# Another order of issue for one recurrent-attention and mixer kernel

## The chip, the core and the metric

The kernel runs on one core of one Trainium2 chip. The metric is the device time of one execution in microseconds (us). Five engines work side by side, each on its own queue and in the order of that queue: TensorE (PE, matmuls), VectorE (DVE), ScalarE (ACT), GpSimd (POOL) and SyncE (SP, which here issues nearly all transfers). They wait for one another by semaphores.

## The reference

Two blocks follow each other: a recurrent attention with a decaying state, and an MLP-mixer block whose input is the attention's output.

```python
def _attn_ref(r, k, v, w, u):          # (4, 8, 768, 48) each, u (8, 48)
    for t in range(S):
        cur = einsum('bhd,bhe->bhde', u[None] * kt, vt)
        y[:, :, t] = einsum('bhd,bhde->bhe', rt, state + cur)
        state = wt[:, :, :, None] * state + einsum('bhd,bhe->bhde', kt, vt)

def _moe_ref(x, w_tok1, w_tok2, w_ch1, w_ch2):     # x (4, 768, 384)
    h = np.maximum(x.transpose(0, 2, 1) @ w_tok1, 0.0) @ w_tok2
    u = x + h.transpose(0, 2, 1)
    return u + np.maximum(u @ w_ch1, 0.0) @ w_ch2
```

## The kernel before

The sequence of 768 steps of each of the 4 batches is cut into three **units** (`UB`) of two chunks of 128 steps, 12 units (`NU`) in all. Unit `i` is a set of **steps** with names, and the texts below write them as `i.name`:

- `ends` and `begins` (DVE): scans over the decay `w`, lines L435 and L443; `keys` and `queries` (DVE, L440 and L446): the keys and queries times these.
- `own0` to `own3` (ACT, L331): the keys times `u`; `own` (PE, L315): their products with the queries; `put` (DVE, L458): the diagonal of these into the tile `at`.
- `tokens` (PE, L345): the keys turned; `copied0`, `copied1` (ACT, L350): the copies of that out of PSUM; `carry` (PE, L365): keys times values into `kv_ps`.
- `by0` to `by3` (ACT, L501) and `up0` to `up3` (in the first three units PE, L508; later DVE): the state carried on over four blocks of 64 steps, each from the one before.
- `gram` (PE, L315) and `mask` (DVE, L327): keys times queries, the part below the diagonal into `at`.
- `before` (PE, L380), `seen` (ACT, L389), `after` (PE, L401): the output from the state and from `at`; `taken0` to `taken2` (ACT, L407): its copy into `x`.
- `small` and `large` (ACT, L427): whether the scan left a range of numbers that is safe.

Beside the units stand the steps of the mixer. Its weights come as words that are taken apart on the chip: `t0` to `t2` are pieces of the first two weights, `c0` to `c8` of the other two, each with `load` (SP, L261), `plus` and `minus` (ACT, L264 and L267), `lead`, `two`, `value`, `sum` (DVE, L270 to L281). The mixer of the first batch is plain: `h0` to `h11` (PE, L947), `relu0` and `relu1` (ACT, L950), `back0` to `back5` (PE, L958, and an addition on DVE, L960), `turn0` to `turn5` (PE, L969, and a copy on ACT, L971), `up` (PE, L993) and `down` (PE, L1004). The mixers of batches 1 to 3 work with split numbers (L667 to L820), take part of the weights from DRAM through a ring of ten slots, and have POOL add one of three forms.

What sets the order is written into the program. The first stage, up to the first three units and `h11`, is one list of steps in a call of `strict`; the rest is merged from ten streams by the digits of the string `ORDER`, a digit naming the stream whose next step comes. `strict` binds every instruction of a step behind the one before it on its engine, so that no scheduler moves it:

```python
for ins in block.instructions[done:]:
    if ins.engine in in_turn:
        if in_turn[ins.engine]:
            tc.add_manual_dep(ins, in_turn[ins.engine], no_sync, reason="order of issue")
        in_turn[ins.engine] = ins.name
```

`behind(gate, f)` makes a transfer wait until the step `gate` has ended. PSUM tiles are few: in the first stage the products `own`, `gram` and `before` share two places (`tag="gram"`), so the third waits until the first has been read, by `put`, `mask` or `taken`. Afterwards six banks go round.

Of the kernel before, what the change touches and what calls it, by code (L numbers as in the profile page):

```python
# [26 lines left out]
UB = C // UC  # L27
NU = B * UB
A = H // 2
# [18 lines left out]
SHRINK = (1.0 - 1.0 / BASE) ** 2  # L48
LEAST, MOST = 2.0 ** -40, 2.0 ** 40
MID = 3 * G // 4 * SEG1  # L50
ORDER = (
    "888008088078808800000888484440800840804080880808804844088488400448088408008888080080884808884040488844488888084840880880"
    "808840880808084448484008800080858808005000458500505588854545558485085848785005080558505855588400558085800005606068606846"
    "860600685786865658688606668086688566668868066800064869889466550048096660988848898089000484488044008000848080000018444141"
    "404040044004000000007000000404000440020000040550000050500000000000000005024200200045005020000555542000002004001224540105"
    "100550500055000750000000055050502000000500004500006624606000520000666506507606600506566660066600060066066606000000000000"
    "006405041104010500004006511611111661096012294296211041111044222990403443439223340234000004000010011000000400000007040000"
    "400040004004000400400000404000055000550000000000000000000005544000050000000000500014511000000000400000004555500545554000"
    "570550000450000000505550060000600066000506665000000665005600000000000066500001666656650661160651610000600006662106266212"
    "191166106100991111112002023393229933300002000001000110000000000000000000000000000000000000000000000000000000000000000000"  # L60
    "00000000000070001011000000000000000000000000000000000000000000000000000000000000000000000000000000000"
)


# [1 line left out]
def rwkv6_then_mixer(  # L66
# [25 lines left out]
    def behind(gate, f):  # L92

        def g():
            done = len(block.instructions)
            f()
            tc.add_manual_dep(block.instructions[done], ended[gate], wait, reason="time of issue")

        return g

    def strict(*fs):

        for f in fs:
            done = len(block.instructions)
            f()
            ended[f] = block.instructions[-1].name
# [5 lines that stand above are left out]
# [66 lines left out]
    def load_w(i):  # L178
        if i < NU:
            for cols in (slice(MID, WCOLS), slice(0, MID)) if i == 0 else (slice(0, WCOLS),):  # L180
                sp.dma_start(w_of(i)[:, cols], w[i][:, cols])
# [4 lines left out]
    def load_part(i, n):  # L186
        for rows in (slice(0, 128),) if i < UB else (slice(0, D), slice(P, P + D)):
            sp.dma_start(rk_of(i)[rows, ts(n, COLS)], rk[i, n, rows, :])

    def load_rk(i):  # L190
        if i < NU:
            for n in (1, 0):
                load_part(i, n)
# [3 lines left out]
    def load_v(i):  # L197
        if i < NU:
            vs[i] = vpool.tile([128, UC, DM], f32, name="vt", tag=f"vt{i % 2}")
            b, j = divmod(i, UB)  # L200
            sp.dma_start(vs[i], v[b, ts(j, UC * 128), :].rearrange("(c p) e -> p c e", p=128))
# [207 lines left out]
    def unit(i):  # L409
# [123 lines left out]
        def each(f, n):  # L533
            return [lambda m=m: f(m) for m in range(n)]

        return dict(ranges=each(ranges, 2), ends=ends, keys=keys, begins=begins, queries=queries, own_u=each(own_u, A),
                    own_gram=own_gram, copied=each(copied, UC), taken=each(taken, 3),
                    own_put=own_put, products=[lambda n=n: products(n) for n in range(3)], sums_put=sums_put,
                    tokens=tokens, gram=gram, mask=mask, carry=carry, before=before, seen=seen, after=after,
                    scaled=[lambda c=c, j=j: scaled(c, j) for c in range(UC) for j in range(2)],  # L540
                    updates=[lambda c=c, j=j: update(c, j) for c in range(UC) for j in range(2)])
# [476 lines left out]
    def attention_pieces(i):  # L1018

        e = units[i]  # L1020
        up, by, sums = e["updates"], e["scaled"], e["products"]
        k = lambda *names: tuple((i, n) for n in names)
        last = lambda *names: tuple((i - 1, n) for n in names) if i > UB else ()

        def piece(f, name, *ops):
            return (i, name), f, ops

        back = i // UB - 2
# [8 lines left out]
        loads = piece(lambda: load_rk(i + 1), "loads", ("Q", 8.0, last("before", "gram", "tokens")))  # L1037
        ends = piece(e["ends"], "ends", ("DVE", 2.6, last("small", "large", "by3", "w")))
        keys = piece(e["keys"], "keys", ("DVE", 1.25, k("ends") + last("loads")))
        small, large = (piece(e["ranges"][n], name, ("ACT", 1.4, k("ends"))) for n, name in enumerate(("small", "large")))  # L1040
        begins = piece(e["begins"], "begins", ("DVE", 2.35, k("ends")))
        tokens = piece(e["tokens"], "tokens", ("PE", 0.9, k("keys") + last("carry"), "k0", "k1"))
        copied = [piece(e["copied"][n], f"copied{n}", ("ACT", 0.6, k("tokens")), ("free", f"k{n}")) for n in range(2)]
# [31 lines left out]
    def interleaved(order, *streams):  # L1075
# [9 lines left out]
    raw_words.append(turned["xT"].rearrange("p m t -> p (m t)").bitcast(u32)[:, :4 * PIECE])  # L1085
    to_tok = conversion(("wtok1", "wtok2"), words_tok, rooms=lambda n: ((0, 1, 3)[n], n % 2))
    to_ch = conversion(("wch1", "wch2"), words_ch, rooms=lambda n: (n % 2, n % 2) if n else (2, 2))
    e0, e1, e2 = (unit(i) for i in range(UB))
    (_, p0, n0, lead0, two0, put0, add0), (_, p1, n1, lead1, two1, put1, add1), (_, p2, n2, lead2, two2, put2, add2) = to_tok
    _, p3, n3, lead3, two3, put3, _ = to_ch[0]  # L1090
    in_turn.update({pe.engine: None, dve.engine: None, act.engine: None, sp.engine: None})
    s0, s1, s2 = (e["updates"] for e in (e0, e1, e2))
    t0, t1, t2 = (e["scaled"] for e in (e0, e1, e2))
    strict(lambda: load_part(0, 1), masks, e0["ends"], e0["own_u"][0], e0["own_u"][1], e0["own_u"][2], e0["own_u"][3], e0["begins"],
           lambda: load_part(0, 0), e0["keys"], lambda: load_part(1, 1), e0["own_gram"], lambda: load_v(0), e0["ranges"][0], lambda: load_w(1),
           e0["tokens"], e0["queries"], e1["own_u"][0], e1["own_u"][1], e0["copied"][0], lambda: load_w(2), e0["gram"], e1["ends"], e0["copied"][1],
           lambda: load_part(1, 0), e0["carry"], e1["own_u"][2], s0[0], e0["own_put"], e1["own_u"][3], e0["ranges"][1], t0[1], s0[1],
           behind(e0["tokens"], to_tok[0][0]), e1["begins"], behind(e1["ends"], lambda: load_part(2, 1)), e1["own_gram"], t0[2], e1["keys"],
           e2["own_u"][0], s0[2], e2["own_u"][1], e1["own_put"], t0[3], e1["tokens"], behind(e0["tokens"], lambda: load_part(2, 0)),
           e0["before"], e2["own_u"][2], e0["mask"], e1["copied"][0], p0, e0["seen"], s0[3], e2["own_u"][3], behind(t0[2], lambda: load_v(1)),  # L1100
           e2["ends"], e1["copied"][1], t1[0], e0["after"], e0["taken"][0], e1["carry"], n0, to_tok[1][0], s1[0], e1["queries"], e0["taken"][1],
           e2["keys"], lead0, t1[1], e2["own_gram"], two0, s1[1], e0["taken"][2], e2["own_put"], e2["tokens"], t1[2], put0, e2["copied"][0],
           s1[2], t1[3], e2["copied"][1], e1["gram"], s1[3], e1["before"], t2[0], p1, add0, lambda: load_v(2), e1["mask"], e2["carry"], e1["seen"],
           h[1], s2[0], h[0], e2["ranges"][0], e2["begins"], behind(t1[1], to_tok[2][0]), t2[1], n1, h[3], e2["queries"], s2[1], lead1, two1,
           e1["after"], t2[2], s2[2], put1, e2["gram"], behind(e1["gram"], to_ch[0][0]), h[2], e1["taken"][0], e1["taken"][1], t2[3], e1["taken"][2],
           behind(t2[3], lambda: load_w(3)), p2, add1, e2["mask"], lambda: load_v(UB), behind(e2["own_gram"], to_ch[1][0]), e2["before"], h[4],
           e2["seen"], n2, e2["after"], lead2, two2, h[5], e2["taken"][0], h[6], e2["taken"][1], put2, e2["taken"][2], h[7], h[8], p3,
           h[10], add2, n3, behind(e1["tokens"], to_ch[2][0]), lead3, two3, rectified[0], h[9], h[11], rectified[1], e1["ranges"][0], e2["ranges"][1], e1["ranges"][1],
           lambda: load_rk(3), put3, lambda: turned["back"](0))

    six_banks.close()
    ps_g, ps_m = None, six_banks.enter_context(tc.tile_pool(name="ps_m", bufs=1, space=bass.MemoryType.PSUM))
# [233 lines left out]
```

## Time and profile before

| | us |
|---|---|
| median of 3 runs (lowest, highest) | 477.70 (477.54, 480.27) |
| profiled execution, its own time | 478.31 |
| its span, first to last instruction | 476.5 |
| PE busy / DVE / ACT / POOL | 459.1 / 344.6 / 265.8 / 54.2 |
| first PE work starts, last PE work ends | 7.59, 471.79 |

The span is 1.8 us shorter than the execution's own time, and the median of the runs is 0.6 us below the profiled one. PE is busy in 96% of the span. The rows of the timeline give the start of an instruction or group from the span's start, its duration, and in brackets how long the engine was idle before it and what ended that.

### The profile page before, as it was taken

Reading aid. Unit: us, or ns where it says so; the run is one execution under the profiler, and the core shown is the slowest. Engines: PE = TensorE matmul, PEld = TensorE weight load, DVE = VectorE, ACT = ScalarE, POOL = GpSimd, SP = SyncE. Lnnn points to the kernel's source line nnn. Section 1 sums busy time; section 2 is a strip of 40 time slices with the busy share of each in tenths; the row PEclk is TensorE's granted clock in tenths of the full one; section 3 lists DMA queues with packets and bytes.
Section 4 is the critical chain, followed back from the end, with each engine's and each line's share of the span. In section 5 each row is a group of like instructions: output and inputs, shape, how many; then the busy total and the mean of one; then the engine's idle time right before and its main releaser. Section 6 shows DMA issues by size and latency. Waiting matters only on the chain.

```text
span 476.5 us, 12778 instructions
## 1 busy us (share of the span) xinstructions
PE 459.1 (96%) x5322; PEld 409.6 (86%) x5322; DVE 344.6 (72%) x495; ACT 265.8 (56%) x606; POOL 54.2 (11%) x58
## 2 busy tenths in 40 slices
PE   3899999999999999999999999999999999999996
PEld 2776588856797668999999999999999999999995
DVE  7998797679598877876897998685587885235341
ACT  6699876674678856453747385351837554134140
POOL 1000000000000001231302002130304003032130
PEclk9999999999999999999999999999999999999999
DMA  8865745573584556963888842754784513336331
GB/s 313 317 221 217 188 169 191 180 275 99 152 228 138 177 179 207 284 186 100 252 283 232 294 154 56 198 173 141 215 227 150 167 61 84 115 101 199 86 99 54
DMA packets 45055, 85.34 MB, mean 179 GB/s; under 512 B 4736, under 2 KB 37376, under 8 KB 44992
## 3 DMA queue, kind: packets, MB, share of 16 engines
q1 hardware_dynamic: 44704, 84.37, 56.3%
q8 instruction: 43, 0.70, 0.6%
q14 instruction: 20, 0.16, 0.1%
q10 hardware_dynamic: 288, 0.10, 0.1%
HBM read 72.65 MB, written 11.80 MB: 177 GB/s over the span
## 4 chain that ended last, share of the span: by engine, by line
PE 90%; ACT 4%; DVE 2%; DMA 2%; issue 1%; SPq 0%; DVEq 0%; ACTq 0%
PE bank L1004 10%; PE bank L772 8%; PE bank L779 8%; PE bank L774 8%; PE bank L790 8%; PE bank L792 8%; PE bank L791 8%; PE bank L993 7%; PE bank L667 3%; PE bank L989 3%; PE bank L726 3%; PE bank L315 2%; PE bank L401 2%; PE bank L380 2%; PE kv_ps L365 2%; PE bank L669 2%
## 5 line engine op out<-in xcount | busy, mean ns | idle before, releaser
L765 POOL TENSOR_TENSOR z_high<-z_high 128x384 fp32r<-128x384 f32 x48 | 52.9, 1107 | 406.7 <-DMA ring<-third 186.8
L754 ACT ACTIVATE z_high<-bank 128x384 fp32r<-128x384 f32 x48 | 23.5, 489 | 58.1 <-PE bank L779 57.7
L772 PE MATMUL bank<-x_forms,forms 128*128 128x384 f32 x216 | 50.3, 341 | 0.0
L779 PE MATMUL bank<-z_more,forms 128*128 128x384 f32 x216 | 50.1, 340 | 0.0
L774 PE MATMUL bank<-x_forms,ring 128*128 128x384 f32 x216 | 49.3, 337 | 0.0
L761 DVE SCALAR_TENSOR_TENSOR z_high<-bank,z_high 128x384 fp32r<-128x384 f32 x48 | 26.5, 554 | 31.4 <-ACT z_high L754 29.4
L1004 PE MATMUL bank<-wch,z 128*128 128x384 f32 x144 | 48.1, 488 | 0.0
L790 PE MATMUL bank<-forms,z_high 128*128 128x384 f32 x140 | 47.8, 342 | 0.0
L792 PE MATMUL bank<-forms,z_high 128*128 128x384 f32 x140 | 47.1, 337 | 0.0
L791 PE MATMUL bank<-ring,z_high 128*128 128x384 f32 x140 | 47.1, 337 | 0.0
L798 DVE SCALAR_TENSOR_TENSOR x<-bank,x 128x384 f32<-128x384 f32 x35 | 18.8, 553 | 39.0 <-PE bank L792 38.9
L1004 PEld LDWEIGHTS bank<-wch,z 128*128 128x128 f32 x144 | 26.8, 190 | 17.2
L501 ACT ACTIVATE before<-state,to_end 112x48 f32<-112x48 f32 x132 | 33.1, 324 | 13.0 <-DVE state L516 7.6
L779 PEld LDWEIGHTS bank<-z_more,forms 128*128 128x128 f32 x216 | 39.0, 188 | 0.1
L772 PEld LDWEIGHTS bank<-x_forms,forms 128*128 128x128 f32 x216 | 38.3, 188 | 0.5
L774 PEld LDWEIGHTS bank<-x_forms,ring 128*128 128x128 f32 x216 | 38.6, 188 | 0.0
L993 PE MATMUL bank<-xT,wch 128*128 128x256 f32 x144 | 32.0, 381 | 0.0
L993 PEld LDWEIGHTS bank<-xT,wch 128*128 128x128 f32 x144 | 27.0, 190 | 3.7
L757 ACT ACTIVATE z_high<-z_high 128x384 fp32r<-128x384 f32 x48 | 25.2, 525 | 3.5
L790 PEld LDWEIGHTS bank<-forms,z_high 128*128 128x128 f32 x140 | 26.3, 188 | 0.2
L791 PEld LDWEIGHTS bank<-ring,z_high 128*128 128x128 f32 x140 | 26.3, 188 | 0.0
L792 PEld LDWEIGHTS bank<-forms,z_high 128*128 128x128 f32 x140 | 26.3, 188 | 0.0
(243 smaller groups left out, 961.2 us busy)
## 6 DMA issues: line engine op xcount, KB each, us to landing
ring<-third SPq DMA_DIRECT2D x144, 192.0 KB, 3.4
raw<-in_words_ch_dram SPq DMA_DIRECT2D x8, 1023.8 KB, 4.8
rk<-in_rk_dram SPq DMA_DIRECT2D x36, 192.0 KB, 5.2
near<-in_near_dram SPq DMA_DIRECT2D x8, 768.0 KB, 5.0
w<-in_w_dram SPq DMA_DIRECT2D x10, 520.5 KB, 5.1
vt<-in_v_dram SPq DMA_DIRECT2D x12, 384.0 KB, 5.0
out_dram<-x SPq DMA_DIRECT2D x17, 192.0 KB, 2.8
third<-forms SPq DMA_DIRECT2D x12, 192.0 KB, 3.3
```

What stands on the lines that cost most here:

```text
L501: act.mul(t[:ROWS, a], state[bt, g][:ROWS, a], by_last(c, j)[:, a:a + 1])
L757: act.mul(z_form(jt, 2), z_form(jt, 0).bitcast(f32), 1.0 / BASE)
L761: dve.scalar_tensor_tensor(z_form(jt, 1), a, 0.0, z_form(jt, 0).bitcast(f32), op0=ALU.max, op1=ALU.subtract)
L765: pool.tensor_add(z_form(jt, 2), z_form(jt, 2).bitcast(f32), z_form(jt, 1).bitcast(f32))
L772: pe.matmul(a, up[m], xf(0)[:, m], start=m == 0, stop=False)
L774: pe.matmul(a, low[:, m], xf(1)[:, m], start=False, stop=False)
L779: pe.matmul(banks["a", jt], joint, xf(2)[:, m], start=False, stop=m == 2)
L790: pe.matmul(a, z[0], up, start=first, stop=False, skip_group_check=True)
L791: pe.matmul(a, z[1], held[bt, s, half, 1, jt], start=False, stop=False, skip_group_check=True)
L792: pe.matmul(a, z[2], joint, start=False, stop=last, skip_group_check=True)
L993: pe.matmul(ps, now["wch1"][:, jt // 4, m, ts(jt % 4, 128)], xT[:, m, ts(s, SEG)], start=(m == 0), stop=(m == DM // 128 - 1))
L1004: pe.matmul(ps, zs[s][:, jt, ts(n, 128)], now["wch2"][:, jt, :], start=(jt == 0), stop=(jt == NJ - 1))
```

## The change

The first stage's list becomes a string `FIRST` of names, with `<gate` for what was `behind`, and it holds another order; `ORDER` gets other digits. The steps, their instructions and their operands are the same; `small` and `large` get names of their own instead of places in a list.

```diff
+FIRST = (
+    "masks 0.ends 0.begins k0 0.own0 0.own1 0.own2 0.own3 r0 0.keys 0.own 0.queries 0.small k1 1.own0 1.own1 1.own2 1.own3 w1 0.tokens "
+    "0.copied1 0.copied0 0.gram 1.ends 1.keys 0.large v0 0.carry 0.up0 1.tokens 0.by1 r1 0.up1 0.by2 w2 t0.load<0.tokens 0.put k2<1.ends "
+    "1.begins t0.plus 1.own 1.put 0.up2 0.by3 0.before 1.copied0 2.own0 1.copied1 r2<0.tokens 0.mask 0.seen 2.own1 v1<0.by2 1.queries 0.up3 "
+    "1.by0 2.own2 2.ends t0.minus t0.lead 2.own3 2.keys 0.after 0.taken1 1.carry 1.up0 1.by1 0.taken0 2.own 2.put 1.up1 1.by2 t0.two "
+    "t0.value t0.sum 1.up2 0.taken2 1.by3 2.tokens 2.copied1 2.copied0 1.before 1.gram 1.mask 1.up3 h0 t1.load t1.plus 2.by0 1.seen t1.minus "
+    "v2 2.carry 2.up0 1.after 2.by1 1.taken0 2.begins 2.queries 2.up1 2.by2 h2 2.up2 t2.load<1.by1 t1.lead t1.two 1.taken1 2.gram 2.by3 "
+    "1.taken2 t2.minus h1 2.mask t1.value 2.before 2.seen h3 h4 t2.plus 2.after 2.taken1 h5 h6 h7 2.taken0 2.taken2 t1.sum c0.load<1.gram "
+    "c0.plus h8 h9 t2.lead t2.two h10 t2.value t2.sum c1.load<2.own c0.minus c0.lead c0.two c0.value h11 relu0 c2.load<1.tokens relu1 back0 "
+    "w3<2.by3 1.large 2.large 1.small rk3 2.small v3"
+)
 ORDER = (
-    "888008088078808800000888484440800840804080880808804844088488400448088408008888080080884808884040488844488888084840880880"
+    "888884408008888880088800000400044888888000088880000048888844448888000888880448000008888888087884008000008448888084444444"
...
-    strict(lambda: load_part(0, 1), masks, e0["ends"], e0["own_u"][0], e0["own_u"][1], e0["own_u"][2], e0["own_u"][3], e0["begins"],
...
+    for name in FIRST.split():
+        name, _, gate = name.partition("<")
+        strict(behind(named[gate], named[name]) if gate else named[name])
```

The change moves later lines by 11, so that L315 of before is L326 of the change.

PE, from the second `gram` of the first stage on. `rk_88` and `rk_89` are the keys and queries of units 0 and 1, `first` those of unit 2. Before:

```order
L315 MATMUL gram<-rk_88 64x64 x32
L365 MATMUL kv_ps<-vt,kT 48x48 x32
L508 MATMUL kv_ps<-before,ident 112x192
L315 MATMUL gram<-rk_89,near 64x64 x32
L508 MATMUL kv_ps<-before,ident 112x192
L345 MATMUL k_ps<-ident,rk_89 128x112 x8
L380 MATMUL y_ps<-before,rk_88 64x48 x24
```

The change:

```order
L326 MATMUL gram<-rk_88 64x64 x32
L376 MATMUL kv_ps<-vt,kT 48x48 x32
L356 MATMUL k_ps<-ident,rk_89 128x112 x8
L519 MATMUL kv_ps<-before,ident 112x192
L326 MATMUL gram<-rk_89,near 64x64 x32
L519 MATMUL kv_ps<-before,ident 112x192
L391 MATMUL y_ps<-before,rk_88 64x48 x24
```

`1.tokens` (`k_ps`, unit 1) now stands right behind `0.carry`, ahead of `0.up1`, `1.own` and `0.up2`, where before it stood behind them.

DVE, at the same place: the tiles `at_92` and `first` of L458 are where `0.put` and `1.put` write. Before:

```order
L436 RECIPROCAL starts<-to_end_93 112x16
L458 TENSOR_TENSOR at_92<-gram,u_rows 128x1024
L443 SCALAR_TENSOR_TENSOR w_90<-w_90,starts 112x1041
L440 TENSOR_TENSOR rk_89<-rk_89,to_end_93 112x1024
L458 TENSOR_TENSOR first<-gram,u_rows 128x1024
```

The change:

```order
L447 RECIPROCAL starts<-to_end_93 112x16
L451 TENSOR_TENSOR rk_89<-rk_89,to_end_93 112x1024
L469 TENSOR_TENSOR at_92<-gram,u_rows 128x1024
L454 SCALAR_TENSOR_TENSOR w_90<-w_90,starts 112x1041
L469 TENSOR_TENSOR first<-gram,u_rows 128x1024
```

`1.keys` moves ahead of `0.put` and `1.begins`.

ACT, from `relu0` and `relu1` to the last `turn` copy ahead of `up`; `junk,flags` are `small` and `large`, the `raw` rows `plus` and `minus` of `c1` and `c2`, `xT` the copies of `turn0` to `turn3`, `near` the steps `own` of unit 3. Before:

```order
L950 ACTIVATE h_145<-h_ps 128x384 x2
L427 ACTIVATE junk,flags<-to_end_93,least 112x1041
L427 ACTIVATE junk,flags<-first,most 112x1041
L427 ACTIVATE junk,flags<-to_end_93,most 112x1041
L264 ACTIVATE raw<-raw,rebias 128x1024
L267 ACTIVATE raw<-raw,rebias 128x1024
L971 COPY xT<-bank_875 128x3x128
L971 COPY xT<-bank_877 128x3x128
L264 ACTIVATE raw<-raw,rebias 128x1024
L267 ACTIVATE raw<-raw,rebias 128x1024
L971 COPY xT<-bank_873 128x3x128
L971 COPY xT<-bank_875 128x3x128
```

The change:

```order
L961 ACTIVATE h_145<-h_ps 128x384 x2
L438 ACTIVATE junk,flags<-to_end_93,most 112x1041
L438 ACTIVATE junk,flags<-first,most 112x1041
L438 ACTIVATE junk,flags<-to_end_93,least 112x1041
L438 ACTIVATE junk,flags<-first,least 112x1041
L275 ACTIVATE raw<-raw,rebias 128x1024
L278 ACTIVATE raw<-raw,rebias 128x1024
L342 ACTIVATE near<-rk_88,u_col 112x2x128 x2
L982 COPY xT<-bank_875 128x3x128
L275 ACTIVATE raw<-raw,rebias 128x1024
L278 ACTIVATE raw<-raw,rebias 128x1024
L982 COPY xT<-bank_877 128x3x128
```

A fourth range step (`2.small`) and two steps `own` of unit 3 come ahead of the first copy, and the second copy comes behind the four `raw` rows instead of ahead of two of them.

More of the change, by code (lines that the diff above doesn't have):

```diff
@@ L50 @@
 MID = 3 * G // 4 * SEG1
-ORDER = (
-    "888008088078808800000888484440800840804080880808804844088488400448088408008888080080884808884040488844488888084840880880"
[L53 to L61, printed above, removed]
@@ new lines @@
+FIRST = (
[9 rows of a table added]
+)
+ORDER = (
+    "088884408008888880088800000400044888888000088880000048888844448888000888880448000008888888087884008000008448888084444444"
+    "008888888888888884884440000044888000458000004487455505588544440558585555555888880000088508555055558880000008005558066666"
+    "586608608586666667650000688800666666866698886666888558800700866668848888000090999490448884408040040488800111448804444800"
+    "004248000440000000000000000000040000444440000055500400000002222424000000040000000000000000422005445550000055000015250005"
+    "555511575000000005005500000000050550000002000050606540052206600006066666005060570005666666606600006600005066065006000001"
+    "405000000166600004440011100040911111226960069122169111111222004440339932234444370000320000000101100004400400000000004400"
+    "004000000000000004444040040004540000044455000000000000400000007000055544000000555500000000115515555555000000005000000500"
+    "000000000000400000050555566650000006660006666000000000006000000050000000565666616666616155600000500166600000122220666161"
+    "191110006699161111122100032332299930000332000000001110000700000000000000000000000000000000000000000000000000000000000000"
+    "00000000000000100001100000000000000000000000000000000000000000000000000000000000000000000000000000000"
@@ L534, in each @@
             return [lambda m=m: f(m) for m in range(n)]
-        return dict(ranges=each(ranges, 2), ends=ends, keys=keys, begins=begins, queries=queries, own_u=each(own_u, A),
+        return dict(small=lambda: ranges(0), large=lambda: ranges(1), ends=ends, keys=keys, begins=begins, queries=queries, own_u=each(own_u, A),
                     own_gram=own_gram, copied=each(copied, UC), taken=each(taken, 3),
@@ L1039, in attention_pieces @@
         keys = piece(e["keys"], "keys", ("DVE", 1.25, k("ends") + last("loads")))
-        small, large = (piece(e["ranges"][n], name, ("ACT", 1.4, k("ends"))) for n, name in enumerate(("small", "large")))
+        small, large = (piece(e[name], name, ("ACT", 1.4, k("ends"))) for name in ("small", "large"))
         begins = piece(e["begins"], "begins", ("DVE", 2.35, k("ends")))
@@ L1087, in rwkv6_then_mixer @@
     to_ch = conversion(("wch1", "wch2"), words_ch, rooms=lambda n: (n % 2, n % 2) if n else (2, 2))
-    e0, e1, e2 = (unit(i) for i in range(UB))
-    (_, p0, n0, lead0, two0, put0, add0), (_, p1, n1, lead1, two1, put1, add1), (_, p2, n2, lead2, two2, put2, add2) = to_tok
-    _, p3, n3, lead3, two3, put3, _ = to_ch[0]
+    first = {i: unit(i) for i in range(UB)}
     in_turn.update({pe.engine: None, dve.engine: None, act.engine: None, sp.engine: None})
-    s0, s1, s2 = (e["updates"] for e in (e0, e1, e2))
@@ L1093, in rwkv6_then_mixer @@
-    t0, t1, t2 = (e["scaled"] for e in (e0, e1, e2))
-    strict(lambda: load_part(0, 1), masks, e0["ends"], e0["own_u"][0], e0["own_u"][1], e0["own_u"][2], e0["own_u"][3], e0["begins"],
[L1095 to L1109, printed above, removed]
@@ new lines, in rwkv6_then_mixer @@
+    named = {"masks": masks, "rk3": lambda: load_rk(3), "back0": lambda: turned["back"](0)}
+    named.update({f"h{n}": f for n, f in enumerate(h)})
+    named.update({f"relu{n}": f for n, f in enumerate(rectified)})
+    for kind, weights in (("t", to_tok), ("c", to_ch[:3])):
+        for n, steps in enumerate(weights):
+            named.update({f"{kind}{n}.{name}": f for name, f in zip(("load", "plus", "minus", "lead", "two", "value", "sum"), steps)})
+    for i, e in first.items():
+        named.update({f"{'rk'[n]}{i}": lambda i=i, n=n: load_part(i, n) for n in range(2)})
+        named.update({f"w{i + 1}": lambda i=i: load_w(i + 1), f"v{i}": lambda i=i: load_v(i)})
+        for name, made in e.items():
+            name = {"own_u": "own", "own_gram": "own", "own_put": "put", "scaled": "by", "updates": "up"}.get(name, name)
+            named.update({f"{i}.{name}{n}": f for n, f in enumerate(made)} if isinstance(made, list) else {f"{i}.{name}": made})
@@ L1111, in rwkv6_then_mixer @@
+    named["v3"] = lambda: load_v(UB)
+    for name in FIRST.split():
+        name, _, gate = name.partition("<")
+        strict(behind(named[gate], named[name]) if gate else named[name])
     six_banks.close()
```

## The prediction

> **What bounds the kernel now.** I read the page's busy table first, then who PE waited for, then stretches, then the timelines of the first 60 us.
>
> ```profile
> PE 459.1 (96%) x5322; PEld 409.6 (86%) x5322; DVE 344.6 (72%) x495; ACT 265.8 (56%) x606; POOL 54.2 (11%) x58
> ...
> PE gram L315 <- DMA rk<-in_rk_dram: 7.6, 1, 7.6
> PE kv_ps L508 <- ACT before L501: 1.4, 3, 1.0
> PE k_ps L345 <- issue: 0.7, 1, 0.7
> PE bank L969 <- ACT raw L267: 0.6, 1, 0.6
> PE bank L401 <- ACT seen L392: 0.6, 2, 0.3
> PE h_ps L947 <- issue: 0.5, 1, 0.5
> PE bank L401 <- issue: 0.5, 1, 0.5
> PE y_ps L401 <- ACT seen L389: 0.4, 1, 0.4
> PE kv_ps L365 <- ACT before L501: 0.4, 1, 0.4
> ...
> 59.10:471.80 412.70, 411.68 (x4292) 374.53 (x4290) 295.16 (x438) 218.52 (x496) 52.89 (x48) 1.00 0.55 170
> ```
>
> PE bounds it. Behind its first 7.6 us, which both kernels spend on the first keys, it idles 5.1 us in all; from 59.1 us (the first `up`) to 471.8 only 1.0 in 412.7. The work is the same in both kernels, so the time after is settled by three things: when the first `up` starts, what waits the new `ORDER` puts in or takes out behind it, and the tail of 4.7 us, which keeps its order.
>
> One more thing hides in PE's busy time:
>
> ```profile
> 13.70 1.50 PE L365 MATMUL kv_ps<-vt,kT 64*48 64x48 f32 x64
> 16.20 0.98 PE L508 MATMUL kv_ps<-before,ident 112*112 112x192 f32 x2 [0.99 <-ACT before L501]
> 17.11 1.99 PE L315 MATMUL gram<-rk,near 48*64 48x64 f32 x64
> 25.56 0.94 PE L365 MATMUL kv_ps<-vt,kT 64*48 64x48 f32 x64 [0.40 <-ACT before L501]
> 30.53 1.16 PE L315 MATMUL gram<-rk 48*64 48x64 f32 x64
> 45.38 3.81 PE L947 MATMUL h_ps<-x,wtok 128*128 128x384 f32 x11 [0.53 <-issue]
> 58.72 0.52 PE L969 MATMUL bank<-ident,x 128*128 128x128 f32 x3 [0.59 <-ACT raw L267]
> ```
>
> The same 64 matmuls of `gram` take 1.99 us at 17.1 and 1.16 at 30.5, `carry` 1.50 at 13.7 and 0.94 at 25.6: PE runs at little more than half speed until between 21 and 23 us, some 6 us after its last long gap (16.2), though the clock column of every window reads 1.00.
>
> **The change part by part.** I walk the first stage with these rows; an instruction's step to the next is a little under its duration, since they overlap.
>
> ```profile
> 13.91 1.16 DVE L458 TENSOR_TENSOR at<-gram,u_rows 128x1024 f32<-128x1024 f32 x1
> 20.30 1.30 DVE L327 COPY_PREDICATED at<-before_it,gram 128x1024 f32<-128x1024 uint8 x1
> 32.06 1.30 DVE L327 COPY_PREDICATED first<-before_it,gram 128x1024 f32<-128x1024 uint8 x1
> 35.60 1.23 DVE L446 TENSOR_TENSOR first<-first,x 112x1024 f32<-112x1024 f32 x1
> 41.00 1.30 DVE L327 COPY_PREDICATED at<-before_it,gram 128x1024 f32<-128x1024 uint8 x1
> 15.27 0.87 ACT L501 ACTIVATE before<-kv_ps,first 112x48 f32<-112x48 f32 x4 [0.80 <-PE kv_ps L365]
> 20.33 0.91 ACT L331 ACTIVATE near<-first,u_col 112x256 f32<-112x256 f32 x2 [2.24 <-DMA first<-in_rk_dram]
> L261 SPq DMA_DIRECT2D raw<-in_words_tok_dram x2: 327/394/460, 12.0 to 18.5; - x2
> ...
> DMA to landing us min/median/max: 6.9/7.1/7.3
> ```
>
> *1.tokens into the gap at 15.2.* Up to 13.7 nothing changes: `carry` ends at 15.2 in both. `1.keys`, now first behind `1.ends` (recip ends 14.0), ends at 15.1 in the place of the row at 13.91, so `1.tokens` (1.65 us at half speed) starts at 15.2, where PE idled 0.99. `0.put` follows to 16.2, and `1.begins`, which took its turn at once before, to 18.4.
>
> *The clock.* PE then has no gap from `0.tokens` at 10.28 on, behind the 0.7 of the waits table's third row. At the 6 us of before, full speed would come at about 16.5; that is worked out from one event. The Trainium skill, "TensorE: Matmul & The Clock Gate", Part 1 (What's actually happening), has the clock opened by one busy window of about 3.4 us out of a free-running row of such windows; by it, an estimate, full speed would come between 13.7 and 17.1. The trace agrees that a start is slow, but took longer than one window from 7.59.
>
> *But it gains little.* With full speed from 16.5 on: `1.tokens` to 16.85, `0.up1` to 17.4, `1.own` to 18.5 (1.09), and on DVE `1.put` to 19.7 and `0.mask` to 20.95. `0.before` takes the PSUM place that `0.mask` reads out, so it can't start sooner. `0.by3` is no earlier: `t0.plus` now stands ahead of it on ACT and its words land at 12.0 + 6.9 = 18.9, then 1.15 and 0.85 give 21.0. PE idles from 19.0 to 20.95, in place of `1.tokens`. `0.before` ends at 21.8, before at 23.0: 1.2 us won. On ACT the wait for `k2`, 2.24 us ahead of the row at 20.33, is gone, since `2.own0` now stands behind `0.by3`. From 21.0 ACT does two copies and two `own` at 0.4, `seen` 0.1 and `1.by0` 0.87, so `1.carry`, which overwrites what `1.by0` reads, starts at 23.65; its row reads 25.56.
>
> *Given back.* `2.tokens` stood between `1.up1` and `1.up2` and filled PE's wait for `1.by2`; now it stands behind both, and PE waits 0.9 us from 27.3 to 28.2. Then come `1.up2` 0.5, `2.tokens` 0.85, and `1.before` (1.1) ahead of `1.gram` (1.1) where it was behind, so `1.gram` ends at 31.8 and `1.mask` on DVE starts at 31.85; its row reads 32.06. `2.begins` and `2.queries` follow as before, and `2.queries` ends at 36.4 where the row at 35.60 ended at 36.8. `2.mask` comes 2.4 us sooner (38.6, row 41.00), but `t1.value` and `t1.sum` stand behind it, and DVE is through with all of them at 42.2 in both kernels. PE ends `2.after` at 42.7 (43.6), then `h5` to `h11`, seven of 0.665 (11 matmuls in the 3.66 us from the row at 45.38 to the next group), to 47.4; before it was 49.1. The 0.53 of issue ahead of the row at 45.38 is left out of this; if it stays, it is 47.9.
>
> *What sets the first up.*
>
> ```profile
> 49.24 0.49 ACT L950 ACTIVATE h<-h_ps 128x384 f32<-128x384 f32 x1 [0.80 <-PE h_ps L947]
> 49.62 1.16 ACT L427 ACTIVATE junk<-to_end,least 112x1041 uint8<-112x1041 f32 x1
> 50.90 1.17 ACT L427 ACTIVATE junk<-first,most 112x1041 uint8<-112x1041 f32 x1
> 53.35 1.20 ACT L264 ACTIVATE raw<-raw,rebias 128x1024 int16<-128x1024 int16 x1
> 55.57 0.83 ACT L971 COPY xT<-bank 128x384 f32<-128x384 f32 x2
> 56.30 1.24 ACT L264 ACTIVATE raw<-raw,rebias 128x1024 int16<-128x1024 int16 x1
> 58.02 0.55 DVE L960 TENSOR_TENSOR x<-x,bank 128x384 f32<-128x384 f32 x1
> 58.56 0.46 ACT L971 COPY xT<-bank 128x384 f32<-128x384 f32 x1
> 59.65 1.70 ACT L331 ACTIVATE near<-rk,u_col 112x256 f32<-112x256 f32 x4
> ```
>
> `up` reads the copies of `turn0` and `turn1`. Before, both were done at 56.4 and PE was held at 58.72 by `turn3`, whose rows of `x` DVE finished at 58.6 (the row at 58.02), behind the `lead`, `two` and `value` of `c1`. Now ACT has ahead of the second copy, from 47.4 on: `relu1` 0.45, four ranges of 1.28 (49.62 to 50.90) 5.1, `c1` twice 1.11 2.2, two of unit 3's `own` 0.85, a copy 0.4, `c2` (56.30 to 58.56) 2.25, a copy 0.45: 11.7 us, so `up` starts at 59.1 to 59.2. The 1.8 us that PE was ahead ends in waits for ACT. Term: **+0.1 us**, and as bounds, from the same rows, -2.6 (ACT holds nothing: PE goes on from 47.4 with six `back` of four matmuls, 1.3 each, and four `turn` of 0.33, to 56.5) and +1.0 (both the 0.53 and half a us of a transfer on top).
>
> *Behind the first up.* The attention's steps move by up to 20 us between the mixer's, but what each waits for moves with it. Three rows name waits there:
>
> ```profile
> 256.17 0.66 PE L401 MATMUL bank<-vt,at 64*64 64x48 f32 x26 [0.45 <-issue]
> 274.07 1.20 PE L401 MATMUL bank<-vt,at 64*64 64x48 f32 x64 [0.28 <-ACT seen L392]
> ```
>
> These two, and one more of 0.28 like the second, make the 1.0 us of the waits table's two rows of L401 on `bank`. The wait of 0.28 at 274.07 is `8.after` behind `8.seen`: they now stand 11.5 us of PE's work apart where it was 1.4, so it goes (-0.28). The third, `11.after`, keeps its neighbours and stays. The first is named issue, which is PE's own queue and no other engine; its place among the instructions moves, and I take it as gone (-0.45), with 0 as the other end. Against these: `hidden` of batch 2 stands half a us nearer to the row forms that it reads from DVE, which were in time by 0.26, so +0.25. Sum behind `up`: **-0.5**; bounds -1.0 (every wait there is gone) and +1.5 (three new ones of the size of the largest).
>
> On the packets themselves: the Trainium skill, "Runtime: NRT & Kernel Launch" (Instruction fetch mechanics), calls the crossing from one block of instructions to the next mostly hidden. By that there is next to nothing to win from them; here the trace has two waits of about 0.5 named issue, 0.2% of the span, and can't tell whether they are of that kind.
>
> **Sum.** Profiled 476.5 + 0.1 - 0.5 = 476.1 of span, 477.9 of execution with the 1.8 around it; the median of the runs lies 0.6 below the profiled one: **477.3 us**, range of this case 474.5 to 480.
>
> **The rivals.** *Full speed all the way (faster).* If full speed comes at once and the waits I put at 19.0 to 20.95 and 27.3 to 28.2 (2.9 us) don't arise, and ACT doesn't hold `up` (2.6), the sum is 5.5 lower: 471.8. For it: 10.28 to 19.0 without a gap. Against it: three separate holds (mask, words, ACT) must all be wrong.
>
> *The clock falls back (slower).* PE's new hole of 2 us at 19 to 21, with another of 0.9 at 27, could keep or put PE at half speed until about 30. The pieces from `0.after` to `1.gram` are 7.6 us at full speed; at 1.99 to 1.16 they are 13.0, 5.4 more, of which the 0.9 is hidden: +4.5 to +5.4, 482.3. It decides if the rows of `gram` behind 25 us still read 1.99. For it: before, a gap of 0.99 at 16.2 preceded six more slow us. Against it: gaps of 0.42 and 0.40 at 24 and 25.6 did nothing. The same page and part of the skill asks for an idle window of about 3.4 us before the clock falls; by it this rival fails.
>
> *It doesn't do what it says.* The waits named issue stay or move to other places: 0.45 and 0.5 more than forecast, 478.3.
>
> **How the numbers follow.** 1% is 4.8 us, about what a measurement of this kernel can tell from no change. The likeliest case has 0.55 and the third rival 0.07, both within 1%. Faster 0.18: the first rival, in whole or in its larger part. Slower 0.20: the clock 0.13, a transfer late in the new SP order 0.07. The range, 472.5 to 482.3, leaves a tenth on each side.
>
> **What would show it.** Right: `1.tokens` at 15.2 behind `carry` with no gap; `gram` of 1.1 to 1.2 us by 20; idle PE ahead of `0.before`; the first `up` at 59 +- 1 behind ACT's copy; PE idle under 1.5 us behind it. Wrong: a first `up` before 57 or after 61; `gram` at 1.99 behind 22 us; a wait over 1 us behind 60.

## The result, and the profile after

The changed kernel took **482.85 us** (median of 7 runs, lowest 482.27) against 478.34 for the kernel before on the same chip: ratio 1.0085, 95% interval 1.0066 to 1.0104. Forecast were 477.3 us and a range of 472.5 to 482.3. The execution that was profiled with the result was a disturbed one (span 490.4 us, clock 0.980), so the rows below come from a second execution of the same kernel, run as the first experiment; its lines are numbered 11 higher than those of before.

The busy row of its page, and then the list of what PE waited for (us in total, times, longest):

```profile
PE 461.5 (96%) x5322; PEld 409.5 (85%) x5322; DVE 342.8 (71%) x495; ACT 267.4 (56%) x606; POOL 53.0 (11%) x58
```

```profile
PE gram L326 <- ACT near L342: 7.6, 1, 7.6
PE bank L980 <- DVE x L971: 1.7, 1, 1.7
PE kv_ps L519 <- ACT before L512: 1.0, 1, 1.0
PE y_ps L391 <- DVE first L469: 0.9, 1, 0.9
PE bank L326 <- issue: 0.8, 1, 0.8
```

Busy PE rose from 459.1 to 461.5. Behind the first `up` only the 0.8 is of any size; two more waits there are 0.15 and 0.28.

And the stretch from the first `up` (60.24) to PE's last work, as the prediction showed it for before; the columns are length, busy time and count of PE, PEld, DVE, ACT and POOL, granted clock, DMA share, GB/s:

```profile
60.24:476.42 416.18, 414.95 (x4290) 375.24 (x4290) 293.69 (x438) 219.32 (x495) 51.71 (x48) 1.00 0.57 171
```

The span is 481.2, 4.7 more than before. The first `up` is 1.16 late (60.24 against 59.08). Behind it the stretch is 3.5 longer (416.18 against 412.70), and PE's idle time in it is only 0.2 more (1.23 against 1.02). **Most of the loss sits inside PE's busy time**: 414.95 against 411.68 for the same matmuls at the same granted clock. No list of waits can name it.

### The profile page after: what moved, and what is told of

Its sections match the earlier page's. It is cut to its first block, busy times and chain, and to the rows that moved or that the text cites. A ratio compares the mean times of both kernels' runs of the same rounds, so it can differ in the third digit from the quotient of the medians.

```text
span 490.4 us, 12777 instructions
## 1 busy us (share of the span) xinstructions
PE 467.4 (95%) x5322; PEld 414.4 (84%) x5322; DVE 342.7 (70%) x495; ACT 267.6 (55%) x606; POOL 52.6 (11%) x58
## 4 chain that ended last, share of the span: by engine, by line
PE 90%; DVE 3%; ACT 3%; issue 2%; DMA 1%; SPq 0%; DVEq 0%; ACTq 0%
PE bank L1015 10%; PE bank L783 8%; PE bank L790 8%; PE bank L785 8%; PE bank L801 8%; PE bank L803 7%; PE bank L802 7%; PE bank L1004 6%; PE bank L737 3%; PE bank L1000 3%; PE bank L326 2%; PE bank L391 2%; PE bank L412 2%; PE kv_ps L376 2%; PE bank L678 2%
## 5 line engine op out<-in xcount | busy, mean ns | idle before, releaser
L776 POOL TENSOR_TENSOR z_high<-z_high 128x384 fp32r<-128x384 f32 x48 | 51.4, 1074 | 422.0 <-ACT z_high L765 193.2
L783 PE MATMUL bank<-x_forms,forms 128*128 128x384 f32 x216 | 51.4, 346 | 0.0
L785 PE MATMUL bank<-x_forms,ring 128*128 128x384 f32 x216 | 50.3, 342 | 0.0
L1004 PE MATMUL bank<-xT,wch 128*128 128x256 f32 x144 | 31.8, 381 | 0.4 <-ACT xT L982 0.4
L1004 PEld LDWEIGHTS bank<-xT,wch 128*128 128x128 f32 x144 | 27.1, 190 | 4.3 <-ACT xT L982 0.7
```

The source lines that it names most:

```text
L776: pool.tensor_add(z_form(jt, 2), z_form(jt, 2).bitcast(f32), z_form(jt, 1).bitcast(f32))
L783: pe.matmul(a, up[m], xf(0)[:, m], start=m == 0, stop=False)
L785: pe.matmul(a, low[:, m], xf(1)[:, m], start=False, stop=False)
L1004: pe.matmul(ps, now["wch1"][:, jt // 4, m, ts(jt % 4, 128)], xT[:, m, ts(s, SEG)], start=(m == 0), stop=(m == DM // 128 - 1))
```

## The experiments

**1. Which half of the change?** One run is the changed kernel again; two cross the halves; the fourth moves four loads.

```diff
 e2:  first stage of before       + ORDER of the change
 e3:  first stage of the change   + ORDER of before
 e4:  the change, with the digit of 9.loads (four loads) moved in ORDER:
-     7.before 8.carry [8.loads' digit: rk of 9] ends7 7.after 8.gram ... ends9
+     7.before 8.carry ends7 7.after 8.gram ... ends9 [rk of 9]
```

> The changed kernel once more, unaltered, for a profile in which the clock column stays near 1.00. Theory P (an instruction packet of TensorE is late): PE again waits 3 to 4 us, named issue, in the gram of unit 8 near 260 us, and the first up starts within 1 us of 60; 4.1 us of extra span divide as about 3.5 behind the first up and under 1 ahead of it. Theory F (the first stage): the first up starts 3 us or more later than the 59.08 of before, and PE idles under 1.5 us behind it. Ratio to before 1.007 to 1.010 under both.

> The first stage of before, the ORDER of the change. Theory P: the wait for the packet belongs to ORDER, so this is as slow as the changed kernel, 1.006 to 1.010 of before. Theory F: the first stage alone is slow, so this is as before or a little faster, 0.998 to 1.001.

> The first stage of the change (FIRST), the ORDER of before. Theory P: within 1 us of before, 0.998 to 1.002, with no wait over 1 us named issue behind 100 us. Theory F: as slow as the changed kernel, 1.006 to 1.010.

> The changed kernel with one digit of ORDER moved: the four loads of keys and queries of unit 9 are issued behind the products of units 7 and 8 (24 digits later), not ahead of them; no instruction of PE, DVE, ACT or POOL moves. Theory P (the packet queues behind these loads): the wait in the gram of unit 8 falls from 3.7 us to under 1, and the time by 2.5 to 3.5 us, 0.993 to 0.995 of the changed kernel, 1.001 to 1.003 of before. Theory F, or a packet that is late for another reason than loads (only the dense run of small matmuls): no change, 1.006 to 1.010 of before.

| | median us | ratio to before (95%) | first up | behind it |
|---|---|---|---|---|
| change again | 483.65 | 1.0133 (1.0088 to 1.0177) | 60.24 | 416.18 |
| first stage of before, new ORDER | 482.64 | 1.0093 (1.0075 to 1.0111) | 60.97 | 416.60 |
| new first stage, ORDER of before | 478.64 | 1.0024 (1.0001 to 1.0047) | 59.41 | 412.59 |
| change, loads moved | 482.37 | 1.0093 (1.0076 to 1.0110) | 59.73 | 416.13 |

`ORDER` carries the loss: with it every kernel takes 416.1 to 416.6 behind the first `up`, without it 412.6 to 412.7. Theory F is out. But theory P is out too: the packet wait in `8.gram` was 0.80, not 3 to 4, and with the loads moved it stayed at 0.81. Its size isn't fixed by `ORDER`: the run with the first stage of before shows 1.32 in the same product, and the execution of 490.4 us 3.75.

So I took each matmul's step, from its start to the next one's start, and compared it with the usual (median) step of its line. In all these kernels the excess sits at the borders between the mixer's matmuls, which use the whole array (128 x 128, or 112 x 128), and the attention's small products `own`, `gram`, `carry`, `before` and `after` (48 or 64 by 48 or 64, in four places of the array). Into a run of small products the last large matmul takes 93 ns longer; out of it the last small one takes 148 ns instead of some 7, and the first large one behind it 106 ns longer (so much later the second one starts): **0.34 us for each unbroken run** (6.11 us over 18 runs before, 9.15 over 27 in the change). `ORDER` of before has 18 such runs behind the first `up`, that of the change 27. Nine more make +3.04 of the +3.47; another 0.2 is idle time. The transposes of `tokens` (L345, 112 x 128) stand between the mixer's matmuls without a price: 323 ns ahead of them, as elsewhere.

The Trainium skill, "TensorEngine Tiling (Array Packing)" (Key Properties), says that changing the tiling mode, not just the tile, drains TensorE. By that rule alone the sign is right; it gives no size. The trace agrees with the sign and has the size, 0.34 us for a way in and out; that it is a drain, the trace can't show.

**2. Make more borders in the kernel before; take some out of both.** Written in the names of the steps:

```diff
 e6, before: nine mixer products pushed into runs, for instance
  up(1,10)
- up(0,11)
  3.carry
+ up(0,11)
  3.gram
 e7, before: runs put together, for instance
- 7.before 8.carry | ends7 joint7 | 8.gram 7.after
+ 7.before 8.carry 8.gram 7.after | ends7 joint7
 e5, the change: the same in seven places, 27 runs to 15
```

> The kernel before, its first stage untouched, with nine single mixer products of ORDER pushed 1 to 3 us later, into the runs of small products: 27 runs instead of 18, nothing else moved. Theory S: 9 x 0.34 = 3.05 us slower, 1.005 to 1.008 of before, with no wait over 0.5 us. Theory W: no new wait, so within 0.5 us, 0.999 to 1.001.

> The kernel before with digits of ORDER moved so that 14 runs of small products are left of 18: the products before of units 6, 9 and 10 (and carry of 7) come later, gram of 8 and after of 7 earlier, beside their neighbours. Theory S: 4 x 0.34 = 1.4 us faster, 0.996 to 0.998 of before, if the steps that wait for the moved ones have the slack that the trace shows (3 us at the least). Theory W: no gain, 0.999 to 1.002.

> In the traces of the changed kernel the small products (gram, carry, before, after: 48 or 64 rows by 48 or 64 columns, four places of the array in turn) stand in 27 unbroken runs behind the first up, before in 18. Each run costs 0.34 us at its borders: the last full matmul ahead of it takes 93 ns more to the next start, the last small one 148 instead of 7 to 16 ns, the second full one behind it 106 ns more. Theory S (switches): this is the changed kernel with digits of ORDER moved so that 15 runs are left; 12 x 0.34 = 4.1 us less, 478.3 us, 0.998 to 1.003 of before; the price of one run stays 0.34. Theory W (single waits and the new neighbours set the loss, not the number of runs): the 0.2 us of visible waits at most, 1.006 to 1.010 of before.

More borders: 481.3 us, 1.0060 (1.0029 to 1.0091), as theory S said, with no wait over 0.3 us behind the first `up` and nothing of the change's in it. The same place in before and then in this run; between the rows lies what a border costs:

```profile
87.70 3.40 PE L993 MATMUL bank<-xT,wch 128*128 128x256 f32 x15
91.03 0.94 PE L365 MATMUL kv_ps<-vt,kT 64*48 64x48 f32 x64
91.78 1.12 PE L315 MATMUL bank<-rk 48*64 48x64 f32 x64
92.84 1.56 PE L993 MATMUL bank<-xT,wch 128*128 128x256 f32 x6
94.24 2.10 PE L1004 MATMUL bank<-wch,z 128*128 128x384 f32 x6
```

```profile
89.68 1.89 PE L993 MATMUL bank<-xT,wch 128*128 128x256 f32 x8
91.50 0.94 PE L365 MATMUL kv_ps<-vt,kT 64*48 64x48 f32 x64
92.36 1.56 PE L993 MATMUL bank<-xT,wch 128*128 128x256 f32 x6
93.86 1.16 PE L315 MATMUL bank<-rk 48*64 48x64 f32 x64
94.95 1.56 PE L993 MATMUL bank<-xT,wch 128*128 128x256 f32 x6
96.35 2.10 PE L1004 MATMUL bank<-wch,z 128*128 128x384 f32 x6
```

From `carry` to L1004 there are 3.21 us before (91.03 to 94.24) and 4.85 here, with six large matmuls more, which take 6 x 0.216 = 1.30: 0.34 is left. No row has a bracket, since PE was never idle. The busy time behind the first `up` says it for the whole kernel, in this run:

```profile
60.84:476.94 416.10, 415.45 (x4292) 374.71 (x4290) 295.37 (x438) 218.68 (x496) 52.88 (x48) 1.00 0.55 169
```

415.45 against 411.68: +3.8, of which 2.97 at the borders. The other 0.8 is scattered in pieces of up to 0.25 and not accounted for.

Fewer borders went the other way than forecast: before with 14 runs 486.9 us, 1.0177 (1.0151 to 1.0204), the change with 15 runs 491.8, 1.0280 (1.0233 to 1.0328). The borders did shrink as counted (6.11 to 4.93 us, and 9.15 to 5.10), but PE's idle time behind the first `up` grew from 1.0 to 8.4, and from 1.2 to 10.1. Busy time did not fall with the borders, since half clock followed some of the waits. The stretches behind the first `up`, in the same columns as above, with 14 runs and with 15:

```profile
59.54:480.71 421.17, 412.79 (x4292) 376.14 (x4290) 295.56 (x438) 218.51 (x496) 52.83 (x48) 1.00 0.54 167
59.35:486.30 426.95, 416.81 (x4290) 379.29 (x4290) 294.82 (x438) 218.73 (x495) 52.79 (x48) 0.99 0.55 166
```

Rows of `after` with 14 runs, then with 15:

```profile
226.81 0.43 PE L401 MATMUL bank<-vt,at 64*64 64x48 f32 x11 [1.28 <-issue]
...
258.16 0.49 PE L401 MATMUL bank<-vt,at 64*64 64x48 f32 x17 [2.62 <-issue]
```

```profile
227.15 0.44 PE L412 MATMUL bank<-vt,at 64*64 64x48 f32 x14 [1.81 <-issue]
...
260.87 0.55 PE L412 MATMUL bank<-vt,at 64*64 64x48 f32 x19 [3.35 <-issue]
```

These four stand in the fourth product of a run of four; with 15 runs two more stand there (2.74 and 1.10), with 14 runs two more in the third (1.42 and 2.50). Each of the two kernels has six runs of four, and the two at 123 and 149 us wait for nothing. The queue that brings instructions shows where the waits come from:

```profile
q8 instruction: 43, 0.70, 0.6%
```

43 packets of 16 KB carry 2 x 5322 matmuls and weight loads. With 14 runs the four waits stand 769, 1792 and 767 of PE's instructions apart, about 3, 7 and 3 times 256: a packet holds some 256 instructions, 128 matmuls. Two small products use one up in about 2 us. In the trace the packets come one after the other, 3.6 us apart where PE waits (224.71 and 228.29 with 15 runs), and PE goes on 1.4 us after one has landed (landed 254.76, 256.76 and 259.42; on at 256.17, 258.16 and 260.87, in before, with 14 and with 15 runs). So a run of four can outrun what is held ahead, though not everywhere. The Trainium skill, "Runtime: NRT & Kernel Launch" (Instruction fetch mechanics), calls the crossing mostly hidden; the mixer's stretches agree, these rows do not.

**3. Runs of three.** The same number of borders in before, cut three and one; and the change with 21 runs, none over three.

```diff
 e9, before:
- 7.before 8.carry | ends7 joint7 | 8.gram 7.after
+ 7.before 8.carry 8.gram | ends7 joint7 | 7.after
 e11, the change:
- 6.after | ten mixer products | 7.carry | three | 7.gram
+ ten mixer products | 6.after 7.carry 7.gram | three
```

> The kernel before with 18 runs of small products as there, but three of them cut otherwise: three products and one (carry 7, before 6, gram 7; before 7, carry 8, gram 8; before 10, carry 11, gram 11) where it was two and two or one and three. The number of borders is the same, so theory S alone gives 478, 0.999 to 1.001. Theory Q (an unbroken run uses up TensorE's instructions at 256 in 2.1 us, faster than packets come, about one in 3.7 us; four products in a row waited 1.3 to 2.6 us): a run of three, 1.05 us shorter, should wait 1.05 us less than a run of four at the same place, 0.2, 1.6 and 1.4 us, 3.2 together, less the 0.45 of before: 480.7, 1.004 to 1.007.

> The changed kernel with 21 runs of small products instead of 27, none of them over three products: after of units 3, 6 and 9 stand beside the next unit's carry and gram, carry and gram of 6 and of 7 side by side, before 10 beside carry 11; nothing of the first stage moves. Theory S: 6 x 0.34 = 2.0 us less than the changed kernel, 480.6 us, 1.004 to 1.007 of before. Theory Q adds that no run of three here should wait over 0.5 us for a packet, except where a load goes out just ahead of it (unit 10 and 11, near 370 us). Theory W (single waits set the loss): no change, 1.008 to 1.010.

Both were slower than expected: 483.1 us (480.0 to 483.6), 1.0092 (1.0055 to 1.0128), and 486.2, 1.0168 (1.0143 to 1.0193). In the first the waits behind the first `up` were none at 226, 0.42 at 256 and 1.59 at 368 (expected 0.2, 1.6, 1.4), and the last one was followed by 6.8 us at half clock:

```profile
368.54 0.45 PE L315 MATMUL bank<-rk 48*64 48x64 f32 x13 [1.59 <-issue]
```

In the second the borders fell from 9.15 to 7.14 us, as the six runs make, and three waits, with 3.4 us at half clock behind the last, took back more:

```profile
227.98 0.45 PE L326 MATMUL bank<-rk 48*64 48x64 f32 x12 [1.44 <-issue]
...
338.77 0.73 PE L326 MATMUL bank<-rk 48*64 48x64 f32 x33 [1.95 <-issue]
```

with 1.19 at 259.85, in a run of two (0.80 in the change). So the border's price holds both ways. Theory Q's limit for three products, 0.5 us, does not: 1.44 and 1.95. The waits fall on the same few instructions in all kernels (near matmul 2892, 3272, 4160 and 4540 of 5322, where a packet ends), and the three waits in runs of three stand in the last product, at one of these. Theory Q's sizes can't be judged from one trace each: the kernel of the fourth experiment was traced twice, and `7.after` waits 1.12 in one trace and not at all in the other. What exactly is held ahead at such a point, and whether other loads than the four that were moved delay it, was not tried.

**4. The end of the first stage.** The first stage of the change, the `ORDER` of before, and the four range activations no longer ahead of `c1` on ACT:

```diff
-    ... relu1 back0 w3<2.by3 1.large 2.large 1.small rk3 2.small v3
+    ... relu1 back0 w3<2.by3 rk3 v3
 and in ORDER's stream of the weights:
- c1.plus c1.minus c1.lead ... c1.sum c2.plus c2.minus ... c2.sum c3.plus
+ c1.plus c1.minus 1.large 2.large c1.lead ... c1.sum c2.plus c2.minus ... c2.sum 1.small 2.small c3.plus
```

> The first stage of the change with the ORDER of before, where PE reached its fourth turn at 57.2 us and waited 1.9 us for ACT and DVE. Here the four range activations of units 1 and 2 (1.3 us each) no longer stand ahead of the conversion c1 on ACT: they become pieces of ORDER, two beside the turns, two behind the first up. Theory T (the queue of ACT and DVE sets the first up): it starts at 57.4 us, 1.7 us ahead of before, and the time is 1.7 to 2.0 us less, 0.995 to 0.998 of before. Theory U (what PE wins ahead of the first up is lost to the next hold): the first up is as early, but waits of 1 to 2 us for ACT or for words come in the first ten us behind it, 0.999 to 1.001.

> As the run with the short tail, and three moves in ORDER: one mixer product between before and after of unit 8 and of unit 11 (they stood side by side and cost 0.48 us, a border costs 0.34), and two more mixer products ahead of gram 8 and after 7, so that the packet that PE waited 0.45 us for has come. Theory S with Q: 20 runs, 0.3 + 0.4 us less than that run, 475.7 us, 0.993 to 0.997 of before. If the borders cost more than the waits that they replace: as that run or slower, 0.996 to 1.000.

> The version with the first stage of the change, the ORDER of before and the four range activations behind the turns, once more: it was 476.9 against 478.1, with an interval too wide to tell. Theory T: first up at 57.9, 1.2 us ahead of before, ratio 0.996 to 0.998. If half clock comes in the first stage as often as it did (it did in a third of the runs), the median is 477 and the ratio 0.998 to 1.000.

The first was 476.86 us against 478.08, 0.9991 (0.9963 to 1.0018); repeated, 476.87 against 478.50, **0.9961 (0.9945 to 0.9978)**: it is ahead of both kernels. The first `up` starts at 57.86 and 57.10 (59.08 before; 58.56 to 60.84 in the other traces with first stage and start of `ORDER` as before). The run with three more moves was 477.6, 1.0004 (0.9985 to 1.0023): it has 20 runs instead of 18 (borders 6.88), the waits at 272 and 378 are gone and none is at 256, and a new one of 0.52 for the last form of `z` has come at 262. Replacing small waits by borders showed no gain.

## Why the prediction was wrong

**The step that failed is the term behind the first up.** It was -0.5, with bounds -1.0 and +1.5; it measured +3.5. The waits in it were not far off: the wait ahead of `8.after` went as said (-0.28), `hidden` of batch 2 waits 0.15 (forecast +0.25), and the packet's wait, taken as gone with 0 as the other end, is 0.80 where it was 0.45 (+0.35). What was missing is a fourth thing beside the three that the prediction says settle the time: how often PE goes from large matmuls to small and back, nine times more in the change, +3.04. The prediction said "the work is the same", counted instructions, and read only brackets of idle time. The rows it needed were in its own trace: the group of six L993 at 92.84 takes 1.40 to the next row, where six steps of 0.216 make 1.30.

**The first up** was forecast 0.1 late and came 1.16 late, 0.3 late with the ORDER of before. The mechanism, ACT's queue from `h11` to its second copy, was right, and so was its sum: 11.7 was forecast, and `up` starts 11.6 behind the end of `h11` in each of the five traces that have the change's first stage and the start of its `ORDER`. It waits for that copy, the second of the three in the last row:

```profile
60.24 2.00 PE L1004 MATMUL bank<-xT,wch 128*128 128x256 f32 x8 [0.45 <-ACT xT L982]
...
59.72 1.21 ACT L982 COPY xT<-bank 128x384 f32<-128x384 f32 x3
```

What was late is `h11`: it ends at 48.6 where 47.4 was forecast, and in this trace the clock had fallen back from 22.7 to 26.1. In the two traces of this first stage in which it did not (15 and 21 runs), `h11` ends at 47.75 and 47.82, and `up` starts at 59.35 and 59.42, 0.3 late.

One hold ahead of that the prediction did not have, at `turn2` and through DVE. Rows of PE, DVE and ACT of the changed kernel:

```profile
57.62 0.55 PE L980 MATMUL bank<-ident,x 128*128 128x128 f32 x3 [1.67 <-DVE x L971]
...
56.41 0.69 DVE L281 TENSOR_TENSOR raw<-raw 128x1024 int16<-128x1024 int16 x1 [3.19 <-ACT raw L278]
57.02 0.55 DVE L971 TENSOR_TENSOR x<-x,bank 128x384 f32<-128x384 f32 x1
...
52.91 1.17 ACT L438 ACTIVATE junk<-first,least 112x1041 uint8<-112x1041 f32 x1
...
54.08 1.21 ACT L275 ACTIVATE raw<-raw,rebias 128x1024 int16<-128x1024 int16 x1
55.19 1.19 ACT L278 ACTIVATE raw<-raw,rebias 128x1024 int16<-128x1024 int16 x1
```

The addition of `back2` stands behind `c1.lead`, which waits 3.19 for `c1.minus`, which stands behind the four ranges. It did not set `up` here, since ACT's copy came later still. The fourth experiment took the ranges away from there, out of both queues, and the `up` came 1.2 to 2.0 us ahead of before.

**The first stage itself** went as worked out in its main steps. Rows of PE:

```profile
15.13 1.31 PE L356 MATMUL k_ps<-ident,rk 112*128 112x112 f32 x8
16.28 0.49 PE L519 MATMUL kv_ps<-before,ident 112*112 112x192 f32 x2
...
19.57 0.67 PE L391 MATMUL y_ps<-before,rk 48*64 48x48 f32 x20 [0.90 <-DVE first L469]
20.70 0.88 PE L391 MATMUL y_ps<-before,rk 48*64 48x48 f32 x28 [0.46 <-ACT before L512]
...
24.03 1.52 PE L376 MATMUL kv_ps<-vt,kT 64*48 64x48 f32 x64
...
26.28 1.16 PE L326 MATMUL gram<-first,near 48*64 48x64 f32 x64
...
28.92 0.58 PE L519 MATMUL kv_ps<-before,ident 112*112 112x192 f32 x2 [0.96 <-ACT before L512]
```

`1.tokens` starts at 15.13 with no gap (forecast 15.2), the record of full clock starts at 15.9 (16.5), `1.carry` starts at 24.03 (23.65), and the wait ahead of `1.up2` is 0.96 (0.9). The hold of `0.before` was read wrongly: 1.95 was forecast, for the place that `0.mask` reads out, but PE waits 0.90 for `1.put` (L469), which ends at 19.52, goes on while `0.mask` runs from 19.42 to 20.73, and then waits 0.46 for `0.by3` on ACT.

**The rivals.** Full speed all the way did not come: all three holds are there, the first of them shorter. The clock did fall back, from 22.7 to 26.1, so that `1.carry` at 24.03 takes 1.52 (0.94 at full speed); but `gram` reads 1.16 at 26.28, so by its own test this rival failed in this trace, and `h11` is 1.2 late, not 4.5. Two other traces show it in full, that of 490.4 us and that with three more moves: 10.2 us at half clock (from 26.9 and 28.7), `gram` at 1.95 (at 32.93 and 34.98), the first `up` at 63.5 and 63.0. That the change doesn't do what it says has a part of the truth: with it the wait named issue behind the first `up` is 0.80, before 0.45. No rival had the borders. And the nine more cuts bought no shorter wait for packets: 0.80, 0.81 and 1.32 in three traces with the change's `ORDER`, 0.45 and 0.34 in two with that of before.

## What to carry to other kernels

Compare busy time as well as idle time, and steps from start to start rather than durations: a pipelined engine can lose 0.7% with no wait in any list. Where products of different tile shapes share TensorE, count the changes of shape as work (0.34 us for a way in and out here), and weigh them against the instruction packets that a long run of tiny matmuls uses up (waits of up to 3.35 us here). And ask of each step on a waiting engine what stands behind it in its queue and who waits for that.

## What the runs showed of the hardware that was not expected

- **The border**, 0.34 us per run of small products, in every kernel: 93 + 141 + 106 ns, medians that agree within 5 ns in before, the change, and the run with nine more.
- **Packets**: runs of four small products waited nothing to 3.35 us, runs of three nothing to 1.95, runs of two nothing to 1.32 in all traces but that of 490.4 us (3.75); large matmuls behind the first `up` never waited for one. PE went on 1.2 to 1.6 us behind the landing.
- **Half clock** begins 0.4 to 1.7 us behind the end of such a wait in the experiments, and comes in whole pieces of 3.4 us. In the change with 15 runs, whose wait ended at 260.87:

```profile
259.43:262.52 3.09, 1.65 (x25) 1.59 (x26) 0.00 (x0) 0.00 (x0) 0.00 (x0) 1.00 0.64 122
262.53:265.93 3.40, 3.40 (x12) 3.40 (x11) 1.63 (x3) 1.80 (x6) 0.35 (x1) 0.50 0.57 174
265.94:269.30 3.36, 3.36 (x20) 3.36 (x20) 3.31 (x6) 2.73 (x8) 2.27 (x2) 1.00 0.46 124
```

  The third column from the end is the clock: 12 matmuls at 0.50 where the next 3.4 us hold 20. Waits of 1.59 (6.8 us at half clock), 1.81, 1.95, 2.50 and 2.74 were followed by it as well; waits of 1.10 to 1.44 and even one of 2.62 were not, nor were those of 1.67 and 1.89 ahead of `turn`. The length of a wait alone doesn't decide it; what does stays open. The Trainium skill, "TensorE: Matmul & The Clock Gate", Part 1 (What's actually happening), asks for one idle window of about 3.4 us before the clock falls; a wait of 1.59 was enough here.
